# New places for the pieces between the products, zero transfers issued by SyncE, routing logits in three split parts

## Chip, cores, metric

The kernel runs as one program on 1 core of a Trainium2 chip. The metric is device time in microseconds (us); lower is better.

## The reference

Three stages follow each other. First a linear attention with decay over 4 batches, 8 heads, 768 steps, head size 48:

```
for t in range(S):
    y[t]  = r[t] @ (state + outer(u * k[t], v[t]))
    state = w[:, None] * state + outer(k[t], v[t])
```

Its output is taken as x with 3072 tokens of 384 numbers. Then a dense stage of width 2048: `x = relu(x @ w_in)**2 @ w_out`. Then a stage with 8 experts of width 1024:

```
logits = x @ w_gate
noisy  = logits + log1p(exp(x @ w_noise)) * noise
top2   = the two largest of noisy per token; their weights by softmax
out    = sum over the two: weight * (relu(x @ w1[e]) @ w2[e])
```

Everything is float32. The order of `noisy` decides where a token goes, so the logits need nearly full precision.

## The kernel before

Five engines work side by side: TensorE (PE) multiplies, VectorE (DVE), ScalarE (ACT) and GpSimd (POOL) do the rest, SyncE (SP) issues most transfers. Each executes its own instructions in the order in which the code writes them, and waits for the others by semaphores.

The dense stage runs over 6 blocks (j = 0 to 5) of 512 tokens, each in 16 steps f of 128 hidden columns. In step f, `mm1(j, f)` makes nine products of 128x512 into a `ph` bank, `gsplit` turns it into g = relu squared in a high and a low part (three ACT operations, then the DVE subtraction `gl`), and `mm2`, two steps behind (LAG = 2), makes nine products into the bank `xo`. Large products use float32 values split into a high and a low part of type fp32r, three products for one.

Between these products stand "slots", two per step: slot 2f after `mm1` and `gsplit` of step f, slot 2f + 1 after that step's `mm2`. `put(n, fn, ...)` puts a piece of other work in slot int(n); the digits behind the point order the pieces of one slot. The tables written out by hand at the top of the file give these numbers:

- `CHUNKS`: attention for the four 128-token chunks q of the next block, eleven pieces each: `pre`, `p_tr` for r and for k, `pre2`, `p_kv`, `p_a`, `p_r` twice, `p_y` twice, `p_x`. `p_y` adds into `vd` on DVE, `p_x` transposes the sum on PE (L484). The lists are for j = 0, j = 1 and j = 2 to 4. Block 5 has no attention.
- the conversion of the dense weights in block 0: piece n (0 to 15; 13 of them in the slots) takes `conv_w1` (an ACT operation), `conv_w2` (four DVE operations, L238, L239, L240, L244, then the load of piece n + 2) and `conv_w3` (an ACT copy, L252, and a POOL subtraction, L253). Piece 14 holds the weights that the `mm2` after slot 28 needs first.
- `ROUTE` and `RESTS`: the routing of block j - 1, in block j: `r_rest`, four `r_row`, the softplus, top 2, rank and eight `r_send`, which scatter the rows by an indirect transfer on POOL. Routing of block 5 stands in the first `up` pieces of the experts, by `ROUTE_LAST`.

`r_row` transposes 128 tokens (three products with `ident`, L559), multiplies them with the gates in plain float32 (L562), copies the logits out on DVE (L564) and the row on ACT (L565, tile `row`), all from one PSUM bank of a ring of three. `finish` copies the block's result to the tile `x2T` on ACT and DVE before that. `rest(eng, out, src)`, used by the attention (L325, L326), subtracts the upper bfloat16 half of a float32 from it and then the upper half of what is left.

`zeros(e)` clears the expert's rows of the buffer `sent` with one transfer of 896 rows of 1,572 bytes, eight in all, in block 1. The experts follow, `up` and `down` pieces on PE, with the weights loaded and split ahead.

Of the kernel before, what the change touches and what calls it, by code (L numbers as in the profile page):

```python
# [10 lines left out]
BF = mybir.dt.bfloat16  # L11
I32 = mybir.dt.int32
AF = mybir.ActivationFunctionType
OP = mybir.AluOpType
AX = mybir.AxisListType
PSUM = bass.MemoryType.PSUM
DRAM = bass.MemoryType.DRAM
P = 128
# [8 lines left out]

CHUNKS = (((0, 1.01, 2.02, 1.03, 3.04, 2.05, 4.06, 4.07, 6.08, 7.09, 8.1),  # L30
# [11 lines left out]
RESTS = (3.4, 3.7, 5.1, 5.2)  # L42

ROUTE = ((5, 6.71, 6.72, 6.73, 6.74, 7.75, 8.76, 9.77, 9.771, 11.27, 12.78, 14.79, 13.8, 17.81, 18.82, 19.83, 20.84,
          25.15, 26.86, 26.87, 27.88),
         (4.7, 6.71, 6.72, 6.73, 6.74, 7.75, 8.76, 9.77, 9.771, 11.27, 12.78, 14.79, 13.8, 17.81, 18.82, 19.83,
          20.84, 24.85, 26.86, 26.87, 27.88),
         (5, 6.21, 6.72, 6.73, 6.74, 6.75, 7.76, 8.77, 8.771, 8.772, 11.78, 12.09, 12.8, 13.81, 13.82, 14.83, 15.84,
          15.85, 15.86, 14.87, 16.88))


ROUTE_LAST = (0.6, 0.6, 0.8, 1.81, 1.8, 1.81, 2.8, 2.81, 2.82, 3.3, 3.8, 4.8, 5.3, 5.81, 4.8, 5.8, 8.8, 7.82, 10.8,
# [11 lines left out]
def body(ctx, tc, r, k, v, w, u, w_in, w_out, w_gate, w_noise, noise, w1, w2, out):  # L64
    nc = tc.nc
# [3 lines left out]
    E, _, F2 = w1.shape  # L69
    NT = B * S  # L70
    KD = DM // P
# [7 lines left out]
    NB = NT // BLK  # L79
# [4 lines left out]
    CAP = NA * P  # L84
    PAD = E * CAP
    UNITS = ((0, 4), (4, 7))
    LAST = UNITS[-1][1]
# [4 lines left out]
    def pool(name, side="left", stack=ctx, **kw):  # L92
        return stack.enter_context(tc.tile_pool(name=name, bufs=1, side=side, reuse_waits="tile", **kw))

    consts = pool("consts")
    eb = pool("eb", side="right")
    dram = pool("dram", space=DRAM)
    sent = dram.tile([PAD + P, XW], F32, name="sent")


    C = {}
# [35 lines left out]
    def bank(tag="att", bufs=3):  # L137
        return ps.tile([P, 512], F32, name=tag, tag=tag, bufs=bufs)
# [118 lines left out]
    pb = bank()  # L257
# [37 lines left out]
    def zeros(e):  # L295
        if e == 0:
            C["zero"] = eb.tile([P, XW], F32, name="zero", tag="s3", bufs=1)
            nc.vector.memset(C["zero"], 0.0)
            nc.vector.tensor_copy(C["zero"][:, XW - 1:], C["part"])
            nc.scalar.dma_start(sent[PAD:, :], C["zero"])  # L300
        nc.scalar.dma_start(sent[e * CAP:e * CAP + LAST * P, :].rearrange("(q p) x -> p q x", p=P),
                            C["zero"][:, None, :].to_broadcast([P, LAST, XW]))

    def zero_out():
# [10 lines left out]
    def upper(ap):  # L315
        return halves(ap)[..., 1]

    def lower(ap):
        return halves(ap)[..., 0]

    def halves(ap):
        return ap.bitcast(BF).rearrange("... (x two) -> ... x two", two=2)

    def rest(eng, out, src):
        eng.tensor_tensor(out, src, upper(src), op=OP.subtract)  # L325
        eng.tensor_tensor(lower(out), out, upper(out), op=OP.subtract)  # L326
# [168 lines left out]
    X2 = {}  # L495

    def mm1(j, f):
        ph = PH[j, f] = bank("ph", 2)
        qi, fo = divmod(f, NF // NP)
        sl = slice(fo * P, (fo + 1) * P)  # L500
        n = 0
        for d in range(KD):
            for wt, xt in ((wih, x1h), (wih, x1l), (wil, x1h)):
                nc.tensor.matmul(ph, wt[qi][:, d, sl], xt[j][:, d, :], start=(n == 0), stop=(n == 3 * KD - 1))  # L504
                n += 1
# [33 lines left out]
    def small(name, shape, dt=F32, bufs=1):  # L539
        return eb.tile([P] + shape, dt, name=name, bufs=bufs)  # L540

    def r_rest(j, i):
        s = RT.setdefault(j, {})
        if i == 0:
            s["row"] = eb.tile([P, TPB, XW], F32, name="row", tag="s6", bufs=2)
            s["noise"] = small("noise", [TPB, E])
            nc.sync.dma_start(s["noise"], noise.rearrange("(q p) e -> p q e", p=P)[:, j * TPB:(j + 1) * TPB, :])

    def r_part(s, i):
        return s["row"][:, i, :DM].rearrange("p (d x) -> p d x", x=P)  # L550

    def r_row(j, i):
        s = RT[j]
        if i == 0:
            s["lz"] = small("lz", [TPB, 2 * E])
        pb = bank()
        x = X2[j][:, :, i * P:(i + 1) * P]
        for d in range(KD):
            nc.tensor.transpose(pb[:, d * P:(d + 1) * P], x[:, d, :], ident)  # L559
        lz = pb[:, KD * P:KD * P + 2 * E]  # L560
        for d in range(KD):
            nc.tensor.matmul(lz, x[:, d, :], C["gates"][:, 0, d, :], start=(d == 0), stop=(d == KD - 1),  # L562
                             skip_group_check=True)
        nc.vector.tensor_copy(s["lz"][:, i, :], lz)  # L564
        nc.scalar.copy(r_part(s, i), pb[:, :KD * P].rearrange("p (d x) -> p d x", x=P))  # L565
        if i == TPB - 1:
            s["lz"] = s["lz"].rearrange("p i (c e) -> p i c e", c=2)

# [388 lines left out]
    AW = 3  # L957
# [31 lines left out]
    for j in range(NB):  # L989
        slots = [[] for _ in range(2 * NF)]  # L990

        def put(n, fn, *args):
            k = int(n)
            slots[k].append((n - k, len(slots[k]), lambda: fn(*args)))

        if j + 1 < NB:
            for i, at_ in enumerate(CHUNKS[min(j, 2)]):
                q = (j + 1) * TPB + i
                todo = [(pre, ()), (p_tr, "r"), (p_tr, "k"), (pre2, ()), (p_kv, ()), (p_a, ()), (p_r, (0,)),
                        (p_r, (1,)), (p_y, (0,)), (p_y, (1,)), (p_x, ())]  # L1000
                for n, (fn, args) in zip(at_, todo):
                    if q > TPB or fn not in (pre, p_tr):
                        put(n, fn, q, *args)
        if j == 0:
            put(0.6, conv_w3, 2)
            for n in range(AW, 2 * NP):
                m = 2 * (n - AW)
                put(m + 0.6, conv_w1, n)
                put(m + 1.6, conv_w2, n)
                put(m + 2.6, conv_w3, n)  # L1010
            put(30.6, load_routing)
        if j == 1:
            for e in range(E):
                put(e + 0.6, zeros, e)
        if j == 2:
            put(2.6, zero_out)
        if j:
            plan = [(r_row, i) for i in range(TPB)] + [(fn,) for fn in (r_soft1, r_soft2, r_soft3, r_top1, r_top2, r_sel, r_w1, r_rank, r_w2)]
            plan += [(r_send, *divmod(i, 2)) for i in range(2 * TPB)]
            for n, (fn, *args) in zip(ROUTE[0 if j == 1 else 1 if j < NB - 1 else 2], plan):  # L1020
                put(n, fn, j - 1, *args)
            for i, n in enumerate(RESTS):
                put(n, r_rest, j - 1, i)
        if j == NB - 1:
            put(4.8, f1_open)
            put(4.8, load_e, 0, 0)
            put(20.8, fetch, 0, 0)
            for n in range(NW):
                put(8.8 + 4 * n, conv_e, 0, n)
                if n + 1 < NW:  # L1030
                    put(8.8 + 4 * n, load_e, 0, n + 1)
            for c in range(KD):
                put(24.8 + 2 * c, turn, 0, 0, c)
            put(30.9, fetch, 1, 0)
        slots = [[p for *_, p in sorted(s, key=lambda x: x[:2])] for s in slots]
        for f in range(NF):
            mm1(j, f)
            gsplit(j, f)
            for p in slots[2 * f]:
                p()  # L1040
            g = j * NF + f - LAG
            if g >= 0:
                mm2(*divmod(g, NF))
                if f == LAG - 1:
                    finish(j - 1)
            for p in slots[2 * f + 1]:
                p()
# [116 lines left out]
```

## Time and profile before

| what | us |
|---|---|
| median of 3 timed runs | 1044.29 |
| lowest and highest of them | 1041.76, 1044.68 |
| the profiled execution's own time | 1036.84 |
| its span from the first to the last instruction | 1035.0 |
| PE busy | 996.3 |
| DVE, ACT, POOL busy | 585.1, 418.5, 397.6 |

The span is what the trace's views cut up; 1.8 us of the execution lie outside it. Busy time of PE is modelled, so its share says where PE pauses, not how near it is to its peak. Granted clock 1.00 is the level of 2.4 GHz; the mean of the run is 0.983. In the views a row names the line of the kernel, the engine, the operation and the tiles as out<-in; idle time stands behind it with what ended it.

### The profile page before, as it was taken

The page shows a single profiled execution, that of the slowest core. Times are in us where ns is not written, and L with a number is a line of the kernel's source. Part 1 is how long each engine was busy: PE and PEld are TensorE (multiplying, and loading weights), DVE is VectorE, ACT ScalarE, POOL GpSimd, SP SyncE. Part 2 cuts the span into 40 slices and gives each one's busy share as a digit, 9 for nine tenths or more (in the row PEclk, how much of TensorE's full clock was granted, in tenths as well). Part 3 has the DMA queues.
Part 4 walks back from the last instruction along what each step waited for, and adds up shares of the span by engine and source line. Part 5 has one row for each costly group of instructions (what it writes and reads, how often), then busy time and mean ns, then how long its engine had stood idle before and what let it go on. Part 6 is the DMA issues. An engine that isn't in the chain of part 4 may idle for free.

```text
span 1035.0 us, 15948 instructions
## 1 busy us (share of the span) xinstructions
PE 996.3 (96%) x6023; PEld 880.0 (85%) x6023; DVE 585.1 (57%) x1070; ACT 418.5 (40%) x731; POOL 397.6 (38%) x435
## 2 busy tenths in 40 slices
PE   8887998999999999999999999999999999999995
PEld 8766876888888888888888899999999898989894
DVE  8998955755964774685254463554545454444320
ACT  2445543334434433443465542443434334434320
POOL 7544543574485467547111253122120312112121
PEclk9888998999999999999999999999999999999998
DMA  8444369446452224322013567376555455554121
GB/s 191 132 136 137 107 181 348 114 106 198 104 126 76 59 67 106 68 64 64 24 58 82 139 142 166 83 141 129 104 104 113 89 117 99 110 98 79 20 32 22
DMA packets 193287, 112.25 MB, mean 108 GB/s; under 512 B 131632, under 2 KB 185776, under 8 KB 193200
## 3 DMA queue, kind: packets, MB, share of 16 engines
q1 hardware_dynamic: 174336, 79.75, 31.9%
q0 software_dynamic: 10624, 19.89, 10.6%
q10 hardware_dynamic: 8240, 11.49, 3.3%
q8 instruction: 49, 0.80, 0.3%
q14 instruction: 38, 0.31, 0.1%
HBM read 74.83 MB, written 36.27 MB: 107 GB/s over the span
## 4 chain that ended last, share of the span: by engine, by line
PE 74%; DVE 15%; ACT 3%; issue 3%; POOL 2%; DMA 1%; ACTq 1%; SPq 0%; DVEq 0%; POOLq 0%
PE ph L798 21%; PE y L819 14%; PE ph L504 13%; PE xo L527 12%; PE y L847 7%; DVE gl L516 2%; DVE t L238 1%; PE att L388 1%; DVE t L240 1%; DVE t L239 1%; DVE am L392 1%; PE att L449 1%; DVE vd L453 1%; DVE t L244 1%; ACT rt L510 1%
## 5 line engine op out<-in xcount | busy, mean ns | idle before, releaser
L830 POOL DMA_INDIRECT out<-yt,id x56 | 87.3, 1559 | 334.1 <-ACT yt L828 291.9
L516 DVE TENSOR_TENSOR gl<-g,gh 128x512 fp32r<-128x512 f32 x96 | 72.2, 752 | 154.8 <-ACT gh L514 154.6
L805 DVE SCALAR_TENSOR_TENSOR hl<-ph,hh 128x512 fp32r<-128x512 f32 (+1 forms) x128 | 75.4, 590 | 145.8 <-ACT hh L804 145.7
L798 PE MATMUL ph<-xh,w0h 128*128 128x320 f32 (+1 forms) x384 | 136.7, 356 | 0.0
L798 PE MATMUL ph<-xh,w0l 128*128 128x320 f32 (+1 forms) x384 | 134.9, 351 | 0.0
L798 PE MATMUL ph<-xl,w0h 128*128 128x320 f32 (+1 forms) x384 | 134.7, 351 | 0.0
L510 ACT ACTIVATE rt<-ph 128x512 f32<-128x512 f32 x96 | 57.1, 595 | 183.4 <-PE ph L504 172.7
L504 PE MATMUL ph<-x1h,wih 128*128 128x512 f32 x288 | 118.9, 413 | 0.0
L527 PE MATMUL xo<-gh,woh 128*128 128x512 f32 x288 | 117.2, 407 | 0.1
L504 PE MATMUL ph<-x1l,wih 128*128 128x512 f32 x288 | 114.5, 398 | 0.0
L504 PE MATMUL ph<-x1h,wil 128*128 128x512 f32 x288 | 114.0, 396 | 0.0
L527 PE MATMUL xo<-gh,wol 128*128 128x512 f32 x288 | 113.3, 393 | 0.0
L527 PE MATMUL xo<-gl,woh 128*128 128x512 f32 x288 | 113.1, 393 | 0.0
L804 ACT ACTIVATE hh<-ph 128x512 fp32r<-128x512 f32 (+1 forms) x128 | 66.1, 517 | 106.3 <-PE ph L798 103.7
L819 PE MATMUL y<-w1h,hh 128*128 128x384 f32 (+1 forms) x280 | 93.7, 335 | 0.0
L819 PE MATMUL y<-w1h,hl 128*128 128x384 f32 (+1 forms) x280 | 93.6, 334 | 0.0
L819 PE MATMUL y<-w1l,hh 128*128 128x384 f32 (+1 forms) x280 | 93.6, 334 | 0.0
L798 PEld LDWEIGHTS ph<-xh,w0l 128*128 128x128 f32 x384 | 72.1, 188 | 8.3
L798 PEld LDWEIGHTS ph<-xl,w0h 128*128 128x128 f32 x384 | 72.2, 188 | 7.2
L798 PEld LDWEIGHTS ph<-xh,w0h 128*128 128x128 f32 x384 | 72.2, 188 | 7.1
L690 POOL DMA_INDIRECT sent<-row,si x48 | 50.2, 1045 | 51.5 <-ACT gh L514 42.4
L779 DVE TENSOR_TENSOR xl<-xt,xh 128x512 fp32r<-128x512 f32 (+1 forms) x48 | 28.4, 592 | 70.3 <-ACT xh L778 70.3
(206 smaller groups left out, 2185.2 us busy)
## 6 DMA issues: line engine op xcount, KB each, us to landing
ws<-in_moe_w SPq DMA_DIRECT2D x128, 96.0 KB, 2.7
ws<-in_moe_w SPq DMA_DIRECT2D x32, 384.0 KB, 3.3
sent<-zero ACTq DMA_DIRECT2D x8, 1375.5 KB, 16.6
G<-sent SPq DMA_DIRECT2D x36, 192.0 KB, 4.7
stg<-in_moe_w_in SPq DMA_DIRECT2D x8, 768.0 KB
stg<-in_moe_w_out SPq DMA_DIRECT2D x8, 768.0 KB, 4.6
out<-zero SPq DMA_DIRECT2D x1, 4800.0 KB, 15.4
lv<-in_v SPq DMA_DIRECT2D x24, 192.0 KB, 2.9
```

The lines of the kernel that those rows point to most:

```text
L504: nc.tensor.matmul(ph, wt[qi][:, d, sl], xt[j][:, d, :], start=(n == 0), stop=(n == 3 * KD - 1))
L510: nc.scalar.activation(rt, ph, AF.Relu)
L516: nc.vector.tensor_tensor(gl, g, gh.bitcast(F32), op=OP.subtract)
L527: nc.tensor.matmul(XO[j][:, d, :], wt[qi][:, fo, sl], gt, start=(f == 0 and n == 0), stop=(f == NF - 1 and n == 2))
L690: st = nc.gpsimd.indirect_dma_start(out=sent, in_=s["row"][:, i, :], in_offset=None, out_offset=bass.IndirectOffsetOnAxis(ap=s["si"][:, i, ...
L779: nc.vector.tensor_tensor(xl[:, c, :], xt, xh[:, c, :].bitcast(F32), op=OP.subtract)
L798: nc.tensor.matmul(ph, wt[:, d, sl], xt[:, d, :], start=(m == 0), stop=(m == 3 * KD - 1))
L804: nc.scalar.activation(hh[:, :n], ph, AF.Relu)
L805: nc.vector.scalar_tensor_tensor(hl[:, :n], ph, 0.0, hh[:, :n].bitcast(F32), op0=OP.max, op1=OP.subtract)
L819: nc.tensor.matmul(py, ht[:, sl], wt[:, fo, :], start=(m == 0), stop=(m == 3 * NF2 - 1))
L830: st = nc.gpsimd.indirect_dma_start(out=out, in_=yt, in_offset=None, compute_op=OP.add, out_offset=bass.IndirectOffsetOnAxis(ap=IDX[e, un] ...
L847: nc.tensor.matmul(py, wt[:, fo, sl], ht[:, :n], start=(m == 0), stop=(m == 3 * NF2 - 1))
```

## The change

New numbers for all slots of the attention, the weight conversion (each of its three parts has a number of its own), the routing and the remainders; both transfers of `zeros` issued by SP, in other slots; and the logits as sums of bfloat16 products. The gates are split once into three bfloat16 parts on POOL (`r_gates`). x is split by `rest` on DVE into the tile `row`, which later takes the row itself. For each of three groups of 128 values there are three products, of 48, 32 and 16 columns; a DVE reduction adds the three groups of 16 columns.

```diff
@@ tables
-CHUNKS = (((0, 1.01, 2.02, 1.03, 3.04, 2.05, 4.06, 4.07, 6.08, 7.09, 8.1),
...
+CHUNKS = (((0.05, 18.86, 0.12, 1.28, 1.7, 0.25, 19.07, 17.86, 2.8, 8.59, 10.62),
+           (1.04, 2.39, 2.87, 11.49, 15.14, 13.05, 12.05, 12.97, 15.15, 16.74, 20.072),
+           (8.9, 10.05, 11.36, 17.63, 17.78, 19.46, 27.09, 24.81, 21.09, 21.79, 26.6),
+           (19.9, 21.94, 23.95, 24.44, 28.47, 24.05, 9.45, 25.8, 28.24, 28.66, 30.23)),
+          ((0.61, 1.15, 1.62, 4.46, 0.92, 4.53, 8.04, 4.78, 9.71, 9.79, 16.75),
+           (8.19, 8.45, 9.21, 10.83, 11.37, 15.55, 15.56, 17.25, 20.81, 22.05, 24.32),
+           (12.48, 15.01, 17.33, 23.4, 25.4, 22.07, 22.34, 22.43, 25.71, 26.15, 28.23),
...
+CONV_AT = ((2.51, 3.49, 5.37),
+           (3.77, 5.56, 6.06),
+           (5.6, 5.79, 6.86),
...
+           (25.17, 25.63, 27.03),
+           (26.63, 27.52, 29.74))
-RESTS = (3.4, 3.7, 5.1, 5.2)
+RESTS = ((3.08, 3.67, 5.03, 7.89),
+         (3.12, 4.23, 4.81, 5.34),
+         (4.06, 5.62, 6.85, 6.88))
...
+ROUTE = ((6.82, 6.85, 7.86, 9.71, 10.44, 11.12, 11.54, 12.03, 12.901, 14.64, 17.23, 17.43, 18.16,
+          27.26, 18.48, 29.39, 18.42, 18.97, 26.19, 31.66, 31.81),
+         (4.66, 6.71, 7.02, 7.36, 8.46, 9.44, 9.66, 10.95, 11.671, 12.52, 14.9, 17.36, 17.83,
+          17.86, 19.95, 29.56, 30.15, 25.55, 26.8, 26.64, 30.69),
...
@@ zeros
-            nc.scalar.dma_start(sent[PAD:, :], C["zero"])
-        nc.scalar.dma_start(sent[e * CAP:e * CAP + LAST * P, :].rearrange("(q p) x -> p q x", p=P),
+            nc.sync.dma_start(sent[PAD:, :], C["zero"])
+        nc.sync.dma_start(sent[e * CAP:e * CAP + LAST * P, :].rearrange("(q p) x -> p q x", p=P),
@@ routing
+    def r_gates():
+        g = C["gates"]
+        rest(nc.gpsimd, g[:, 1], g[:, 0])
+        C["gates3"] = consts.tile([P, KD, 3, 2 * E], BF, name="gates3")
+        for n, t in enumerate((upper(g[:, 0]), upper(g[:, 1]), lower(g[:, 1]))):
+            nc.gpsimd.tensor_copy(C["gates3"][:, :, n, :], t)
...
     def r_rest(j, i):
...
+        rest(nc.vector, r_part(s, i), X2[j][:, :, i * P:(i + 1) * P])
...
-        lz = pb[:, KD * P:KD * P + 2 * E]
+        lz = pb[:, KD * P:KD * P + 6 * E].rearrange("p (g e) -> p g e", g=3)
         for d in range(KD):
-            nc.tensor.matmul(lz, x[:, d, :], C["gates"][:, 0, d, :], start=(d == 0), stop=(d == KD - 1),
-                             skip_group_check=True)
-        nc.vector.tensor_copy(s["lz"][:, i, :], lz)
-        nc.scalar.copy(r_part(s, i), pb[:, :KD * P].rearrange("p (d x) -> p d x", x=P))
+            for n, t in enumerate((upper(x[:, d, :]), upper(xr[:, d, :]), lower(xr[:, d, :]))):
+                nc.tensor.matmul(lz[:, n:], t, C["gates3"][:, d, :3 - n, :], start=(d == 0 and n == 0),
+                                 stop=(d == KD - 1 and n == 2), skip_group_check=True)
+        nc.vector.tensor_reduce(s["lz"][:, i, :], lz.rearrange("p g e -> p e g"), axis=AX.X, op=OP.add)
+        nc.scalar.copy(xr, pb[:, :KD * P].rearrange("p (d x) -> p d x", x=P))
@@ main loop
-                m = 2 * (n - AW)
-                put(m + 0.6, conv_w1, n)
-                put(m + 1.6, conv_w2, n)
-                put(m + 2.6, conv_w3, n)
+                for at_, fn in zip(CONV_AT[n - AW], (conv_w1, conv_w2, conv_w3)):
+                    put(at_, fn, n)
...
+            put(2.9, r_gates)
             for e in range(E):
-                put(e + 0.6, zeros, e)
+                put(e * 3 // 2 + 3.6, zeros, e)
```

## Rows read from the trace of the kernel before

**Rows 1.** The page's busy table: us (share of the span) xinstructions.
```profile
PE 996.3 (96%) x6023; PEld 880.0 (85%) x6023; DVE 585.1 (57%) x1070; ACT 418.5 (40%) x731; POOL 397.6 (38%) x435
```

**Rows 2.** Busy time by stretch; blocks 0, 1, 2, 5, then experts; columns in first line.
```profile
core 0: us, PE busy (x) PEld busy (x) DVE busy (x) ACT busy (x) POOL busy (x), PEclk, DMA share, GB/s
37.00:138.40 101.40, 90.41 (x484) 74.70 (x483) 89.38 (x99) 53.51 (x84) 50.12 (x34) 0.91 0.45 125
138.40:236.40 98.00, 91.50 (x588) 76.19 (x588) 56.56 (x121) 35.80 (x64) 53.06 (x57) 0.97 0.66 191
236.40:325.00 88.60, 87.67 (x589) 73.23 (x588) 57.15 (x122) 35.60 (x64) 52.28 (x55) 1.00 0.49 134
...
500.50:570.20 69.70, 69.70 (x328) 57.78 (x327) 28.56 (x78) 38.86 (x66) 9.31 (x15) 1.00 0.21 55
570.20:600.00 29.80, 29.80 (x160) 25.84 (x160) 17.14 (x53) 16.67 (x30) 7.41 (x6) 1.00 0.54 130
600.00:1010.00 410.00, 410.00 (x2387) 386.97 (x2386) 191.93 (x299) 155.62 (x283) 93.38 (x122) 1.00 0.51 102
```

**Rows 3.** Waits of PE, whole run: us in total, times, longest us.
```profile
PE att L484 <- DVE vd L425: 10.1, 2, 5.8
```

**Rows 4.** Timeline of ACT in block 1: start us, us, instruction [idle before <-releaser].
```profile
162.76 4.18 ACTq L301 DMA_DIRECT2D sent<-zero  x1
...
166.98 0.48 ACT L565 COPY row<-att 128x384 f32<-128x384 f32 x1 [3.08 <-DVE lv L326]
```

**Rows 5.** Timeline of PE in block 1.
```profile
167.51 1.17 PE L437 MATMUL att<-Z,rT 112*128 112x96 f32 x4 [4.85 <-ACT row L565]
```

**Rows 6.** Timeline of PE in block 5: gate products, then the next row.
```profile
516.42 0.74 PE L562 MATMUL att<-gates,x2T 128*128 128x16 f32 x6
517.01 0.52 PE L559 MATMUL att<-ident,x2T 128*128 128x128 f32 x3
```

**Rows 7.** Timeline of PE in block 5: the rank piece and what follows.
```profile
531.28 0.19 PE L663 MATMUL att<-sel,mask 128*128 128x32 bf16 x1
531.32 0.18 PE L665 MATMUL att<-pre,ones 128*128 128x32 bf16 x1
531.35 0.17 PE L667 MATMUL att<-tot,ones 128*128 128x8 bf16 x1
531.37 0.48 PE L527 MATMUL xo<-gh,woh 128*128 128x512 f32 x1
531.69 0.40 PE L527 MATMUL xo<-gl,woh 128*128 128x512 f32 x1
531.92 0.39 PE L527 MATMUL xo<-gh,wol 128*128 128x512 f32 x1
```

**Rows 8.** DMA queues from 146 to 185 us: packets, MB, share of 16 engines.
```profile
q10 hardware_dynamic: 7440, 11.47, 86.4%
```

**Rows 9.** Groups of DVE instructions, whole run: xcount | busy us, mean ns | idle before.
```profile
L326 DVE TENSOR_TENSOR lv<-lv 128x384 bf16<-128x384 f32 x16 | 9.6, 598 | 0.5
L325 DVE TENSOR_TENSOR lv<-lv 128x384 f32<-128x384 f32 x16 | 8.8, 550 | 0.0
```

**Rows 10.** Groups of POOL instructions in block 0.
```profile
L253 POOL TENSOR_TENSOR wol<-t,woh 128x768 fp32r<-128x768 f32 x8 | 15.0, 1881 | 24.4 <-ACT woh L252 24.4
```

**Rows 11.** Groups of DVE instructions in block 0.
```profile
L238 DVE TENSOR_SCALAR t<-t 128x768 f32<-128x768 f32 x14 | 19.4, 1388 | 4.0 <-ACT t L231 4.0
L240 DVE SCALAR_TENSOR_TENSOR t<-stg,t 128x768 int32<-128x768 int32 x14 | 17.0, 1214 | 0.5
L244 DVE SCALAR_TENSOR_TENSOR t<-stg,t 128x768 int32<-128x768 int32 x14 | 15.5, 1105 | 0.5
L239 DVE TENSOR_SCALAR t<-t 128x768 int32<-128x768 int32 x14 | 13.6, 975 | 0.5
```

**Rows 12.** Timeline of DVE in block 0: its first gl, the last conversion's last operation.
```profile
43.08 0.69 DVE L516 TENSOR_TENSOR gl<-g,gh 128x512 fp32r<-128x512 f32 x1 [0.45 <-ACT gh L514]
...
130.69 0.96 DVE L244 SCALAR_TENSOR_TENSOR t<-stg,t 128x768 int32<-128x768 int32 x1
```

**Rows 13.** One line, L238: duration ns min/median/max, first and last start us.
```profile
L238 DVE TENSOR_SCALAR t<-t x16: 542/1485/2183, 23.8 to 126.9; 128x768 f32<-128x768 f32 x16
```

More of the change, by code (lines that the diff above doesn't have):

```diff
@@ L25 @@
 CONV = {2: 0, 3: 1}
-CHUNKS = (((0, 1.01, 2.02, 1.03, 3.04, 2.05, 4.06, 4.07, 6.08, 7.09, 8.1),
[11 rows of a table removed]
-RESTS = (3.4, 3.7, 5.1, 5.2)
[L44 to L49, printed above, removed]
+CHUNKS = (((0.05, 18.86, 0.12, 1.28, 1.7, 0.25, 19.07, 17.86, 2.8, 8.59, 10.62),
[11 rows of a table added]
+CONV_AT = ((2.51, 3.49, 5.37),
+           (3.77, 5.56, 6.06),
+           (5.6, 5.79, 6.86),
+           (7.44, 7.69, 8.35),
+           (8.33, 9.36, 11.19),
+           (9.67, 11.86, 13.47),
+           (12.66, 13.68, 15.85),
+           (15.34, 15.72, 16.16),
+           (17.06, 17.88, 18.34),
+           (19.88, 19.95, 21.52),
+           (21.26, 23.6, 24.17),
+           (25.17, 25.63, 27.03),
[4 more added lines that the diff above has]
+ROUTE = ((6.82, 6.85, 7.86, 9.71, 10.44, 11.12, 11.54, 12.03, 12.901, 14.64, 17.23, 17.43, 18.16,
[5 rows of a table added]
 ROUTE_LAST = (0.6, 0.6, 0.8, 1.81, 1.8, 1.81, 2.8, 2.81, 2.82, 3.3, 3.8, 4.8, 5.3, 5.81, 4.8, 5.8, 8.8, 7.82, 10.8,
@@ L556, in r_row @@
         pb = bank()
-        x = X2[j][:, :, i * P:(i + 1) * P]
+        x, xr = X2[j][:, :, i * P:(i + 1) * P], r_part(s, i)
         for d in range(KD):
             nc.tensor.transpose(pb[:, d * P:(d + 1) * P], x[:, d, :], ident)
-        lz = pb[:, KD * P:KD * P + 2 * E]
+        lz = pb[:, KD * P:KD * P + 6 * E].rearrange("p (g e) -> p g e", g=3)
         for d in range(KD):
-            nc.tensor.matmul(lz, x[:, d, :], C["gates"][:, 0, d, :], start=(d == 0), stop=(d == KD - 1),
-                             skip_group_check=True)
-        nc.vector.tensor_copy(s["lz"][:, i, :], lz)
-        nc.scalar.copy(r_part(s, i), pb[:, :KD * P].rearrange("p (d x) -> p d x", x=P))
+            for n, t in enumerate((upper(x[:, d, :]), upper(xr[:, d, :]), lower(xr[:, d, :]))):
[3 more added lines that the diff above has]
+        nc.scalar.copy(xr, pb[:, :KD * P].rearrange("p (d x) -> p d x", x=P))
         if i == TPB - 1:
@@ L1021, in body @@
                 put(n, fn, j - 1, *args)
-            for i, n in enumerate(RESTS):
+            for i, n in enumerate(RESTS[0 if j == 1 else 1 if j < NB - 1 else 2]):
                 put(n, r_rest, j - 1, i)
```

18 rows, old and new, of tables (CHUNKS, ROUTE) are left out of this document.

## The prediction, made before the change was run

> **What bounds the kernel now.** I read the page's busy table first: TensorE (PE) is busy 96% of the span [rows 1]. A share that high hides stages with different limits, so the next view was the table of busy time by stretch, cut at the first product of each 512-token block [rows 2]. The reader is to see four things there. From 600 us to 1010 us PE never pauses, and block 5 and the stretch after it are full too. Block 2 idles 0.93 us in 88.6. Block 0 lasts 101.4 us with PE busy 90.4 at a granted clock of 0.91, and VectorE (DVE) busy 89.4: it is the one block that DVE sets. Block 1 does the same work as block 2 and lasts 98.0, 9.4 us longer, at clock 0.97. So there are three places to win or lose: block 0, the 9.4 us of block 1, and PE's own work everywhere else. Which wait ends last in each came from the waits of PE: its longest is the transposes of p_x (L484) for the sum `vd` (L425) that stands behind the weight conversions in DVE's queue [rows 3]. In block 1 the timeline shows ScalarE (ACT) held by its own transfer issues: one `sent<-zero` issue takes 4.18 us, the row copy waiting behind it starts at 166.98, and PE, which needs that copy's PSUM bank, idles 4.85 us until 167.51 [rows 4, 5]. PE then pays again: clock 0.97 over 98 us is 2.9 us of work lost, where block 2 has 1.00 [rows 2].
>
> **Gate products.** Each of 24 row pieces now multiplies x with the gates in true float32: three products in the source, six records in the trace. They run from 516.42 to 517.01, 0.59 us [rows 6]. The change has nine bf16 products of 48, 32 or 16 columns. The nearest bf16 rows are those of the rank piece: from start to start 0.03 us and 0.02 us at 32 columns, and 0.02 us at 8 [rows 7]; the width does not show, so nine cost some 0.23. The first float32 product behind them takes 0.32 instead of 0.23 to the next one: 0.09 more, and the way in a further 0.01 [rows 7]. So 0.59 becomes 0.33, and 24 x 0.26 = 6.2 us goes, nearly all in blocks where PE is the bound. Ends: without the 0.09 it is 24 x 0.36 = 8.6; with it paid twice 24 x 0.17 = 4.1. I take 6.2, the row's own pattern.
>
> A rule of the Trainium skill speaks against this term: "TensorE: Matmul & The Clock Gate", section "LDWEIGHTS (loading the stationary operand)", gives a weight load about P/1.2 ns for P columns, an estimate of 107 ns for 128 columns whatever they hold. The six float32 records agree with it (590/6 = 98 ns). Nine loads by it would be 0.96 us, and the edit would cost 24 x 0.37 = 9 us in place of gaining 6. The bf16 rows, at 20 to 30 ns with a 128-column load each, say otherwise [rows 7], and the same page's fast weight load for types other than fp32 goes with them.
>
> **The zero transfers.** They leave ACT's queue for SyncE's (SP's) and go from slots 0.6 to 7.6 to slots 3.6 to 13.6. ACT loses the blocked issues, and with them the wait that ends last in block 1. I set the block to block 2's 88.6: 9.4 us gone. Bounds: 0, if the wait only changes its engine, and 10.3, if block 2's 0.93 of idle goes as well. The transfers are no smaller: ACT's queue moved 11.47 MB from 146 to 185 us [rows 8], so about 3 MB per 10 us, and the engines were full. What is behind the zeros on SP? In issue order it is the noise load, zeros 0 to 3, the load of k for chunk 11, then r and the eight turned loads for chunk 10. SP does not keep step with PE, so the first four (each 896 rows of 1,572 bytes, 1.4 MB; together some 19 us) go in one burst from slot 3.6, about 8 us into the block, to about 27 us. The loads behind them cannot start before about then anyway: they wait for DVE's transposes of chunk 9 in slots 8 and 9. Their first user is chunk 10 in slots 12 to 15, about 36 to 43 us in. Chunk 9's loads are issued at slot 1.6, ahead of every zero. That is the cover; without it the queue of loads slips by up to 4 us for each zero before it.
>
> The Trainium skill, "DMA: Bandwidth & Descriptors", section "Issuing engines are not separate DMA queues", says that the issuer changes only who spends the issue time, on the same 16 engines. By that rule the 9.4 us come back only so far as the issue on ACT was the cause, which the 4.85 us wait supports; the rest is the second rival below.
>
> **DVE's remainders.** r_rest now has two subtractions for each of the 24 row pieces. Operations of the same 128x384 shapes take 0.55 and 0.60 us [rows 9]: 4.6 us a block, 27.6 in all. In blocks 1 to 4 DVE rises from some 57 to 62 us of 88, in block 5 from 29 to 33 of 70, in the first `up` pieces (570 to 600 us) from 17 to 22 of 30 [rows 2]. The cost is nothing on PE as long as that idle time covers it; the first of them waits for ACT's last copy of x2T, behind it stand the chunk's mask products and `gl`, and PE's row piece comes one and a half slots later. The reduction that replaces the copy of `lz`, and five small GpSimd operations once, stay under 1 us off the path; at the price of GpSimd's 1.88 us subtraction [rows 10] the five would be 9.4 us of a GpSimd that has 45 idle us in block 1 [rows 2].
>
> **New places in block 0.** No work goes away. A conversion's four DVE operations are 1.39 + 0.98 + 1.21 + 1.11 = 4.69 us [rows 11], and 13 of them (61 us) with some 27 us of attention work and `gl` fill DVE. PE cannot pass slot 28 before the weights of piece 14 are converted. Summing DVE's work slot by slot at those durations, the old order has 77.6 us up to that conversion (slot 23) and 84.9 to the last one (slot 25); the new has 79.1 (slot 25) and 85.1 (slot 27). Both start from the first `gl` at 43.1 [rows 12]. In the old order the last conversion ends at 131.65 [rows 12]: 43.1 + 84.9 = 128.0, so 3.7 us of gaps, and PE needs 6.7 us more. In the new order the first conversion comes later (slot 3, not 1), but a(4), kv(4) and a transposed chunk are done in that time; I count 0.6 us lost. The last conversion ends at 43.7 + 85.1 = 128.8 without gaps. `gl`, Z and `vd` are 2 us more, then the transposes of p_x (0.5), and nine products at 0.23 (2.1): 133.4. The weights of piece 14, converted by 122.8 and finished by a ScalarE copy and GpSimd's 1.88 [rows 10], come earlier than that. The p_x pieces now stand two slots behind their y where it was one, which attacks the 10.1 us of rows 3. Gaps of 1.6, somewhat under half of the old, give 135.0, a gain of 3.4 us. Bounds: if half of the excess of the conversions over the shortest run of one (0.54 for the first operation [rows 13], so at least 0.85 x 13 = 11) goes too, the gain is some 9; if the gaps double to 7.4, the block ends at 140.8, a loss of 2.4.
>
> **Blocks 2 to 5 and after** keep their PE work but for the gates. Block 2's idle 0.93 is all that new places can win there; late remainders can cost as much. I take zero. The rest of the program has the old code.
>
> **Sum.** 6.2 + 9.4 + 3.4 = 19.0 us. The profiled execution took 1036.84 us (span 1035.0 and 1.8 around it), so its like would take 1017.8. The timed runs lie at 1041.76 to 1044.68, median 1044.29, that is 7.4 above the profiled one; carried over, the forecast is 1025.3, so 1025.
>
> **Rivals.**
> 1. Block 0 is won more fully: fewer conversions run beside GpSimd's work, and PE's clock stays up. For it: the first operation ranges from 0.54 to 2.18 us [rows 13]. Against: GpSimd's subtraction still follows each conversion. Gain 9 more: 1016. Chance 0.17.
> 2. The loads queue behind the zeros on SP and block 1 keeps its length, the wait moved from ACT to DVE's transposes. For: full transfer engines [rows 8]. Against: the order of issue above. 1025 + 9.4 = 1034. Chance 0.14.
> 3. Slower: the remainders come too late. DVE takes them in order behind ACT's copy; if PE reaches its first row piece before they are done, it waits up to 4.6 us in each of blocks 1 to 5, 23 us, 4 more than the sum: 1048. It decides from the point where DVE is over 4 us behind PE in slot 4. Against: DVE has 31 us to spare in block 2 [rows 2]. Chance 0.07.
> 4. The change does not do what it says: gates cost as much as before (0.59) and block 1's wait moves, leaving block 0 alone: within 0.3%, about 1042. Chance 0.05.
>
> The forecast has 0.57, with 1018 to 1033 as its own range. The range of 1012 to 1039 takes in the first two rivals and their unknowns and leaves out the last two and the tails, some 0.18. What a measurement of this kernel can tell from no change is 0.3%, 3.1 us. Faster: 0.57 + 0.17 + 0.14 = 0.88; same 0.05; slower 0.07.
>
> **What would show it.** In the profile after: bf16 gate products at 20 to 30 ns from start to start, and a row piece 0.26 us shorter; no ACT issue of zeros, block 1 near 88 us with clock 1.00; block 0 near 98; DVE busier by some 27 us in all with PE idle in blocks 2 to 5 under 1 us each. The prediction is wrong if row pieces wait for remainders, if block 1's first 40 us hold a PE wait for a transposed chunk, or if block 0 keeps its 101.

## The result, and the profile after

The changed kernel takes 1029.63 us (median of 4 runs, 1029.01 to 1030.97) where the kernel before takes 1043.56 (4 runs, 1041.76 to 1044.68): a ratio of 0.987, 95% interval 0.985 to 0.989, 13.9 us faster. The forecast was 1025, so 19 us; the time lies inside the range. The profiled execution after has a span of 1027.2, 7.8 less than the profiled one of before.

Busy time by stretch after, cut as in [rows 2]: blocks 0, 1, 2, 5, the first expert pieces, the experts behind them (us, PE, PEld, DVE, ACT, POOL, granted clock, DMA share, GB/s):

```profile
37.00:132.00 95.00, 89.55 (x484) 72.67 (x482) 86.26 (x99) 54.23 (x84) 48.63 (x33) 0.94 0.44 128
132.00:226.50 94.50, 88.11 (x601) 73.47 (x600) 65.90 (x131) 35.52 (x63) 56.83 (x63) 0.98 0.72 202
226.50:315.50 89.00, 86.83 (x600) 72.00 (x601) 62.76 (x130) 35.76 (x63) 52.74 (x56) 1.00 0.48 134
...
488.90:563.80 74.90, 73.43 (x358) 59.52 (x358) 33.50 (x87) 38.89 (x67) 9.49 (x17) 1.00 0.25 62
563.80:603.10 39.30, 36.88 (x220) 32.55 (x219) 31.16 (x76) 19.86 (x34) 14.06 (x12) 1.00 0.53 126
603.10:1000.00 396.90, 395.62 (x2307) 373.42 (x2305) 183.14 (x281) 152.01 (x276) 88.52 (x116) 1.00 0.52 101
```

The next table cuts every kernel of this study at the same products: a block runs from its first product to the next block's; "experts 1" is the first expert's `up` pieces and its first `down`, where the last routing stands.

```
us                     blk0   blk1   blk2   blk3   blk4   blk5  experts1   rest*    span
before                101.4   98.0   88.6   87.2   88.3   73.8    37.3    423.3   1035.0
after                  95.1   94.4   89.0   86.8   86.7   74.9    39.3    424.1   1027.2
a0_changed_again       94.3   95.2   89.8   86.8   86.6   75.9    40.5    423.8   1031.4
e1_zero_behind_v       94.5   90.7   88.0   85.8   86.7   75.1    40.4    424.4   1025.6
e2_zeros_on_act        94.8   97.1   88.1   85.8   86.6   75.4    40.4    424.1   1030.3
e3_old_gates           94.5   91.9   87.7   86.5   87.4   78.0    37.3    423.5   1024.7
e4_sends_early         94.5   95.1   88.1   85.8   86.6   75.4    40.3    424.0   1027.4
b1_block0_places       94.2  100.0   89.7   89.1   89.3   73.8    37.3    423.3   1034.1
b2_split_gates_alone  100.7   98.7   91.0   90.6   91.1   72.4    40.6    422.6   1045.5
b3_zeros_on_sp_alone  101.3   94.7   89.6   89.0   89.4   73.8    37.3    423.3   1035.4
c1_three_waits_mended  94.0   90.6   89.1   86.9   86.6   72.4    41.0    424.0   1021.5
c2_old_gates_mended    94.6   91.9   89.5   87.6   87.8   73.8    37.3    423.5   1022.4
d1_old_gates_last      94.2   91.2   89.9   86.9   86.6   72.4    37.3    422.8   1018.1
d2_no_gpsimd_split     94.0   90.5   89.8   87.5   86.6   72.4    41.1    423.6   1022.9
* what follows experts 1; ahead of block 0 lie 36.4 to 39.9 us
```

So block 0 gave 6.3 us and block 1 only 3.6; blocks 2 to 4 together 1.6; block 5 lost 1.1, experts 1 lost 2.0 and the rest 0.7. The waits of PE after (us in total, times, longest) name the losses. The 10.1 us of [rows 3] are gone; the 3.5 us of `xo` for `woh` and `wol` are new, in block 0, where `mm2` waits for its first converted weights:

```profile
PE att L688 <- DVE am L408: 4.7, 1, 4.7
...
PE att L583 <- ACT row L590: 2.8, 4, 0.9
PE xo L543 <- ACT woh L268: 2.2, 1, 2.2
...
PE xo L543 <- POOL wol L269: 1.3, 1, 1.3
...
PE att L587 <- DVE row L342: 1.2, 2, 0.8
```

**Block 1.** SP's timeline after (start us, us, instruction): the first four zero transfers go in one burst, as forecast, but the fifth stands ahead of the load of v for chunk 10.

```profile
147.04 7.15 SPq L317 DMA_DIRECT2D sent<-zero  x4
...
169.52 0.43 SPq L317 DMA_DIRECT2D sent<-zero  x1
170.05 0.51 SPq L183 DMA_DIRECT2D lv<-in_v  x1
170.60 2.00 SPq L317 DMA_DIRECT2D sent<-zero  x1
```

DVE takes its instructions in order, and the routing chain that PE's rank piece (L688) needs stands behind v's subtraction. DVE's timeline after, then PE's:

```profile
176.24 0.56 DVE L341 TENSOR_TENSOR lv<-lv 128x384 f32<-128x384 f32 x1 [4.55 <-DMA lv<-in_v]
...
182.22 0.16 DVE L656 TENSOR_TENSOR tot<-pre,sel 128x8 bf16<-128x8 bf16 x1
```

```profile
183.99 0.18 PE L688 MATMUL att<-sel,mask 128*128 128x32 bf16 x1 [4.72 <-DVE am L408]
...
185.03 0.63 PE L520 MATMUL ph<-x1h,wih 128*128 128x512 f32 x1
185.46 0.63 PE L520 MATMUL ph<-x1l,wih 128*128 128x512 f32 x1
```

The releaser that the waits name is `am`, the next operation in DVE's queue behind `tot`, probably for the PSUM bank that it reads; all of this queue stands back by the 4.55 us for v. Behind the pause two products start 0.43 us apart instead of 0.23, at the lower clock level, 1.2 GHz: the mean granted clock from 184 to 188 us is 0.58.

**Gate products.** PE's timeline in block 5 after: nine bf16 products, and the products that follow them; then a float32 row piece of before in the same place.

```profile
511.91 0.19 PE L587 MATMUL att<-gates,x2T 128*128 128x48 bf16 x1
511.93 0.20 PE L587 MATMUL att<-gates,row 128*128 128x32 bf16 x2
...
512.09 0.20 PE L587 MATMUL att<-gates,row 128*128 128x32 bf16 x2
512.14 0.47 PE L520 MATMUL ph<-x1h,wih 128*128 128x512 f32 x1
512.45 0.39 PE L520 MATMUL ph<-x1l,wih 128*128 128x512 f32 x1
```

```profile
513.34 0.74 PE L562 MATMUL att<-gates,x2T 128*128 128x16 f32 x6
513.93 0.48 PE L504 MATMUL ph<-x1h,wih 128*128 128x512 f32 x1
514.24 0.40 PE L504 MATMUL ph<-x1l,wih 128*128 128x512 f32 x1
```

Nine take 0.23 us, 25 ns from start to start, in place of the 0.59 of [rows 6]. The first large product behind them takes 0.31 to the next one instead of 0.23, but so does the one behind the float32 gate products of before (513.93 to 514.24). So a row piece gains 0.36, not the 0.26 of the forecast, which charged that step to the new products alone. Block 5 bears it out: where PE does not pause, it takes 73.8 us with old gates (before) and 72.4 with split ones (b2, c1, d1), and 4 x 0.36 = 1.4. The 107 ns that the prediction worked out from "TensorE: Matmul & The Clock Gate" of the Trainium skill, section "LDWEIGHTS (loading the stationary operand)", is not what such a product costs here: the record of each of these weight loads lasts 0.10 us, but they start 25 ns apart.

**Remainders.** Groups of DVE after, whole run: the same shapes as [rows 9], at a mean of 0.73 and 0.82 us, and up to 1.4 and 2.1.

```profile
L342 DVE TENSOR_TENSOR row<-row 128x384 bf16<-128x384 f32 x24 | 19.6, 816 | 0.8
L341 DVE TENSOR_TENSOR row<-x2T 128x384 f32<-128x384 f32 x24 | 17.6, 733 | 3.3 <-ACT x2T L550 3.3
```

**Block 5.** The expert's fetch of its rows (SP's timeline) is issued at 542.86, and DVE waits for it:

```profile
542.86 2.71 SPq L786 DMA_DIRECT2D G<-sent  x4
```

```profile
549.61 1.06 DVE L801 STREAM_TRANSPOSE xt<-G 128x512 f32<-128x512 f32 x1 [3.76 <-DMA G<-sent]
```

### The profile page after: what moved, and what is told of

Same layout as the page of the kernel before. It is cut to its first block, busy times and chain, and to the rows that moved or that the text cites. A ratio compares the mean times of both kernels' runs of the same rounds, so it can differ in the third digit from the quotient of the medians.

```text
span 1027.2 us, 16145 instructions
## 1 busy us (share of the span) xinstructions
PE 986.9 (96%) x6095; PEld 868.5 (85%) x6095; DVE 623.2 (61%) x1118; ACT 419.9 (41%) x731; POOL 406.4 (40%) x440
## 4 chain that ended last, share of the span: by engine, by line
PE 77%; DVE 10%; issue 4%; ACT 3%; DMA 2%; POOL 2%; SPq 1%; another core or an unknown queue 0%; ACTq 0%; DVEq 0%; POOLq 0%
PE ph L823 19%; PE ph L520 16%; PE y L844 14%; PE xo L543 13%; PE y L872 6%; PE att L404 2%; PE att L465 1%; DVE t L254 1%; DVE gl L532 1%; DVE t L256 1%; DVE t L255 1%; PE att L453 1%; PE att L482 1%; DMA ws<-in_moe_w 1%; ACT rt L526 1%
## 5 line engine op out<-in xcount | busy, mean ns | idle before, releaser
L532 DVE TENSOR_TENSOR gl<-g,gh 128x512 fp32r<-128x512 f32 x96 | 82.3, 857 | 106.8 <-ACT gh L530 95.3
L715 POOL DMA_INDIRECT sent<-row,si x48 | 49.9, 1039 | 64.8 <-ACT w0h L763 41.1
```

Of the source, the lines that this page charges most:

```text
L532: nc.vector.tensor_tensor(gl, g, gh.bitcast(F32), op=OP.subtract)
L715: st = nc.gpsimd.indirect_dma_start(out=sent, in_=s["row"][:, i, :], in_offset=None, out_offset=bass.IndirectOffsetOnAxis(ap=s["si"][:, i, ...
```

## The experiments

Theory after the result: the mechanisms of the forecast work, and three new waits take some 10 us back: v behind a zero transfer in block 1, remainders of the split gates on a DVE that shares time with GpSimd, and a late fetch in block 5. Rivals: ACT's freedom comes from the spread slots, not from the new issuer; the split gates gain and the places alone lose; the profiled before is not typical of its timed runs. Ratios are to the kernel before, run beside each group. In the group of e1 to e4 that kernel took 1037.03 (1036.33 to 1038.47), not 1043 to 1044 as in the others, so those four are compared with each other.

**e1.** Zero transfers 4 to 7 go behind the load of v in their slots.

```
-                put(e * 3 // 2 + 3.6, zeros, e)
+                put(e * 3 // 2 + (3.6 if e < 4 else 3.85), zeros, e)
```

> Zeros 4 to 7 stand behind the v load of chunk 10 in SyncE's order (slot 9.85 instead of 9.6); nothing else is changed. Theory: in the changed kernel VectorE waited 4.55 us for that v load, which stood behind zero 4, the routing chain behind it was late, and TensorE waited 4.72 us at the rank piece and then ran at half clock. Then the wait at the rank goes and block 1 (94.5 us) falls to 88 to 90, the time to 1024. Rival: the rank is late because VectorE has 4.6 us of remainders more in front of it; then block 1 keeps 94 us and the time 1029.6.

Measured 1026.56, ratio 0.989 (0.988 to 0.991). The forecast of this run was a little too good (88 to 90 and 1024). DVE's wait for v and PE's for the rank in e1:

```profile
176.49 0.56 DVE L341 TENSOR_TENSOR lv<-lv 128x384 f32<-128x384 f32 x1 [2.39 <-DMA lv<-in_v]
```

```profile
PE att L688 <- DVE am L408: 1.4, 1, 1.4
```

Block 1 falls to 90.7, against 95.1 in e4, whose block 1 is the changed kernel's; timed, e1 is 3.9 below e4. In the changed kernel, four transfers' place in SP's queue cost about 4 us.

**e2.** The changed kernel with the same slots, the zeros issued by ACT.

```
-            nc.sync.dma_start(sent[PAD:, :], C["zero"])
+            nc.scalar.dma_start(sent[PAD:, :], C["zero"])
```

(and the same for the main transfer.)

> The changed kernel with the zero transfers issued by ScalarE again, in the new slots. Theory: the issuing engine is what mattered in block 1, so ScalarE is held by issues of up to 4 us again and block 1 is 98 us or more, the time 1033 or more. Rival: the new slots alone, spread over 11 instead of 8, free ScalarE, and the loads on SyncE no longer stand behind zeros: block 1 at 90 or less, the time 1025.

Measured 1031.42, ratio 0.994 (0.993 to 0.996). ACT's timeline, then DVE's, in e2:

```profile
158.58 0.71 ACTq L317 DMA_DIRECT2D sent<-zero  x1
...
177.57 0.99 ACTq L317 DMA_DIRECT2D sent<-zero  x2
```

```profile
180.31 1.41 DVE L341 TENSOR_TENSOR lv<-lv 128x384 f32<-128x384 f32 x1 [5.65 <-DMA lv<-in_v]
```

An issue holds ACT 0.4 to 0.7 us, not the 4.18 of [rows 4]: the later slots, spread over 11 instead of 8, freed ACT, whoever issues the transfers. v is late all the same, by 5.65, though no zero stands ahead of it in SP's queue: SP issues it at 176.74 (170.05 after), and its own waits put 4.6 us before that down to zero transfers. So each was half right: ACT is free, as the rival had it, and block 1 is as long as the theory nearly had it, from another cause. "DMA: Bandwidth & Descriptors" of the Trainium skill, section "Issuing engines are not separate DMA queues", has the issuer change only who spends the issue time; e2 agrees, 1031.4 against the 1030.4 of e4, where SP issues.

**e3.** The changed kernel with the float32 gate product of before and without remainders.

```
-        rest(nc.vector, r_part(s, i), X2[j][:, :, i * P:(i + 1) * P])
...
-            for n, t in enumerate((upper(x[:, d, :]), upper(xr[:, d, :]), lower(xr[:, d, :]))):
...
+            nc.tensor.matmul(lz, x[:, d, :], C["gates"][:, 0, d, :], start=(d == 0), stop=(d == KD - 1),
```

> The changed kernel with the float32 gate products and no remainders; places and zeros as changed. Theory: 24 row pieces are 0.36 us longer on TensorE (8.6 us), and the waits that remainders bring go (0.6 to 0.8 us a block in blocks 2 to 4, 2.0 in the experts' first pieces, something in block 1): net 2 to 4 us slower than the changed kernel, 1032 to 1034. Rival: VectorE's 27.6 us of remainders cost as much as the products give, so the time stays at 1029 or falls.

Measured 1026.70, ratio 0.990 (0.989 to 0.992): 3.7 us below e4, where the theory wanted it slower. Against e4 it wins 3.2 in block 1 and 3.0 in experts 1 and loses 0.7 and 0.8 in blocks 3 and 4 and 2.6 in block 5. In the changed kernel the split gates cost more than they bring. In block 1 the wait at the rank is nearly gone, with v still behind the fifth zero transfer:

```profile
PE att L686 <- DVE am L408: 1.5, 1, 1.5
```

That is the rival of e1, remainders ahead of the rank in DVE's queue. Each of the two, moving v (e1, 90.7) or taking the remainders away (e3, 91.9), mends most of block 1; both together (c2, 91.9) bring no more than e3 alone. The loss needed both.

**e4.** Block 5's eight sends in slots 15.6 to 17.1 instead of 16.5 to 20.4.

> The changed kernel with the eight sends of block 5 in slots 15.6 to 17.1 instead of 16.5 to 20.4. Theory: the last send set the start of the first fetch, so the turned tokens came late (VectorE waited 3.76 us for G, ScalarE 5.58 behind it) and the last products of the dense stage lost 2.4 us: the time falls by 2 to 2.5 us to 1027.3. Rival: the fetch is limited by the transfers themselves or the wait costs TensorE nothing: 1029.6.

Measured 1030.43, ratio 0.994 (0.992 to 0.995). The first send starts 41.6 us into the block, as it did after, the fetch is issued at 54.1 (after: 53.9), and DVE still waits for it in e4:

```profile
548.92 1.06 DVE L801 STREAM_TRANSPOSE xt<-G 128x512 f32<-128x512 f32 x1 [4.25 <-DMA G<-sent]
```

The theory falls in this form: the new slots did not move the sends at all, presumably because the top-2 and rank pieces before them still stand at slots 14.98 and 15.16.

**a0.** The changed kernel again.

> The changed kernel again, unaltered, on the chip of the runs it is compared with. Both theories: ratio to the kernel before 0.987 as first measured. Rival: the ratio depends on how slow the first blocks of the kernel before are on that chip (its time was 1043.6 in one call and 1037.0 in the next), then 0.992 to 0.994.

Measured 1032.09 (1030.0 to 1033.17), ratio 0.988 (0.987 to 0.990): the result repeats. A before near 1037, the rival's condition, did not come up beside it.

**b1.** The kernel before with the changed `CHUNKS[0]` and `CONV_AT` alone.

> The kernel before with the new places of block 0 alone (attention chunks 4 to 7 and the conversions). Theory: the 6.3 us by which block 0 became shorter (101.4 to 95.1) come from these places: block 0 at 95, block 1 at 98, time 6 us below before. Rival: block 0 gained from something else, as an other state of TensorE's clock; then under 3 us.

Measured 1036.82, ratio 0.994 (0.992 to 0.995): block 0 at 94.2, so its gain comes from these places. DVE's conversions in block 0, in the changed kernel (xcount, busy, mean ns, idle before):

```profile
L256 DVE SCALAR_TENSOR_TENSOR t<-stg,t 128x768 int32<-128x768 int32 x14 | 16.0, 1146 | 0.5
L254 DVE TENSOR_SCALAR t<-t 128x768 f32<-128x768 f32 x14 | 15.7, 1122 | 1.4 <-ACT t L247 1.4
L255 DVE TENSOR_SCALAR t<-t 128x768 int32<-128x768 int32 x14 | 14.8, 1060 | 0.5
L260 DVE SCALAR_TENSOR_TENSOR t<-stg,t 128x768 int32<-128x768 int32 x14 | 14.8, 1058 | 0.5
```

They sum to 4.39 us a conversion where [rows 11] have 4.69: 14 x 0.30 = 4.1 us; and the idle time ahead of the first operation is 1.4 instead of 4.0. But `gl` got longer (a mean of 0.82 instead of 0.68) and waits more (5.9 instead of 1.3), so this is not the block's gain. PE's own account is: of 101.4 and 95.0 us it idles 11.0 before and 5.5 after, and its busy time falls from 90.4 to 89.6 at a clock of 0.94 instead of 0.91. How much of that the shorter conversions brought is not shown.

**b2.** The kernel before with split gates and remainders alone, in the old places. **b3.** The kernel before with the zeros on SP in the new slots alone.

> The kernel before with the split gates and the remainders alone. Theory: TensorE's row pieces are 0.36 us shorter, but the old places give the remainders too little time: row 0 stands at slot 4.7 with rests at 3.4 to 5.2; blocks 1 to 5 gain under 4 us, the first expert pieces lose 2 to 4: within 2 us of before. Rival: the gain is 6 us as worked out before the run.

> The kernel before with the zero transfers on SyncE in the new slots alone. Theory: ScalarE is no longer held, so the 4.85 us wait goes with its half clock; the loads of chunk 10 stand behind zeros in another order than in the changed kernel: block 1 from 98 to 89 to 92, time 6 to 9 us below before. Rival: the wait moves to the loads and block 1 stays above 95.

b2 took 1047.79, ratio 1.0035 (1.002 to 1.005): slower by 3.4 us, more than the 2 that its theory allowed. Waits of PE in b2:

```profile
PE att L571 <- DVE row L326: 7.9, 8, 1.3
...
PE att L571 <- DVE row L325: 1.8, 4, 0.6
```

Row pieces do wait for remainders there, 9.7 us in 12 waits: rival 3's mechanism, at less than half of its price. b3 took 1037.31, ratio 0.993 (0.992 to 0.995), block 1 at 94.7: between its theory and its rival. PE waits there for `vd` (3.1 us) and `kT` (1.3), and for no load. The transfers' part is worth 3.3 us of block 1 against the profile of before, 5.3 against b1's, and 7 us timed.

**c1, c2, d1, d2: mending the waits.** c1 is the changed kernel with e1's move, block 5's routing in its old slots with remainders early, and the last four remainders earlier. c2 is c1's places with e3's old gates (without that last move).

```
-         (4.06, 5.62, 6.85, 6.88))
+         (3.08, 3.1, 4.2, 4.3))
...
-         (6.42, 8.08, 8.31, 9.32, 9.72, 10.18, 10.35, 10.54, 10.581, 10.902, 12.54, 15.16, 14.98,
+         (5, 6.21, 6.72, 6.73, 6.74, 6.75, 7.76, 8.77, 8.771, 8.772, 11.78, 12.09, 12.8, 13.81, 13.82, 14.83, 15.84,
...
-ROUTE_LAST = (0.6, 0.6, 0.8, 1.81,
+ROUTE_LAST = (0.6, 0.6, 0.61, 0.62,
```

> The changed kernel with three small moves: zeros 4 to 7 behind the v load; the routing of block 5 in the old, earlier places, with its remainders in slots 3 and 4; the remainders of the last routing issued together before the first split. Theory: three waits go: 3.7 us in block 1, 2.4 at the end of the dense stage (fetch later than the turn's slot because the rank stands at slot 15), 2 at the first expert pieces: 8 us below the changed kernel, 1021. Rival: GpSimd still stretches VectorE's remainders (2.11 us for one of 0.60) and the fetch is late for another reason: only block 1 gains, 1025.

> The changed kernel with float32 gates and no remainders, zeros 4 to 7 behind the v load, block 5's routing in the old places. Theory: with the waits mended the split gates are worth their 6 us on TensorE, so this one is 3 to 6 us slower than the one with split gates and the same moves. Rival: remainders cost what the products give, so both are within 1 us or this one is faster.

Both took 1025.0 (1025.05 and 1024.97, both 0.982, 0.981 to 0.984). That is the time of both rivals, though c1 mended block 5 as well as block 1; only experts 1 did not gain. The fetch in block 5 is issued 48.7 us into the block in c1 instead of 53.9, and the block falls to 72.4. Between c1 and c2, split gates win 5.0 us in blocks 1 to 5 (20 row pieces at 0.36 are 7.2; PE waits 2.0 for row copies, L583, that c2 does not have) and lose 3.7 in experts 1. There PE waits 3.4 us for remainders and row copies in c1, and the granted clock of the stretch is 0.96; in c2 it never pauses there and has 1.00. Why the remainders are late: GpSimd's timeline in c1, then DVE's.

```profile
559.56 6.26 POOL L764 TENSOR_TENSOR w1l<-ws,w1h 128x768 fp32r<-128x768 f32 x3 [29.42 <-ACT w1h L763]
```

```profile
559.85 2.20 DVE L341 TENSOR_TENSOR row<-x2T 128x384 f32<-128x384 f32 x1
562.08 2.07 DVE L342 TENSOR_TENSOR row<-row 128x384 bf16<-128x384 f32 x1
564.04 2.18 DVE L341 TENSOR_TENSOR row<-x2T 128x384 f32<-128x384 f32 x1
566.26 0.59 DVE L342 TENSOR_TENSOR row<-row 128x384 bf16<-128x384 f32 x1
```

As long as GpSimd's three subtractions run, each remainder lasts as long as one of them (6.26 / 3 = 2.09); the one behind them takes 0.59. d2 gives GpSimd's share of the expert weights to DVE, d1 is c1 with the old gates and no remainders in the last routing alone (and its last remainders' move undone, which is then empty).

```
-SPLIT_POOL = 4
+SPLIT_POOL = 0
```

```
-        rest(nc.vector, r_part(s, i), X2[j][:, :, i * P:(i + 1) * P])
+        if j < NB - 1:
+            rest(nc.vector, r_part(s, i), X2[j][:, :, i * P:(i + 1) * P])
...
+        if j == NB - 1:
```

> The mended version with split gates everywhere, and the low parts of the first four expert weights computed on VectorE (0.96 us each) instead of GpSimd (1.8 us). Theory: GpSimd's subtractions stretch VectorE's remainders (0.55 to 2.2 us); without them the remainders take 0.55 and 0.60, VectorE has 3.8 us more, and the first eight expert pieces take 38 to 39 us instead of 41.0. Rival: the remainders are late by their place in VectorE's queue; then with 3.8 us more work there it gets worse, 42 us or more.

> The kernel with the mended waits, split gates in blocks 1 to 5, float32 gates without remainders in the last routing alone. Theory: the split gates pay some 5 us in blocks 1 to 5 and lose 3.7 us in the experts' first pieces and 0.7 behind them, so this one is 4 us below both mended versions: 1021 where before is 1043.6, ratio 0.978. Rival: the loss in the first pieces comes from somewhere else than the last routing's remainders: 1025, ratio 0.982.

d2 took 1025.45, ratio 0.982 (0.981 to 0.984). DVE's remainders in d2 and a wait of PE:

```profile
561.97 0.55 DVE L341 TENSOR_TENSOR row<-x2T 128x384 f32<-128x384 f32 x1
562.55 0.59 DVE L342 TENSOR_TENSOR row<-row 128x384 bf16<-128x384 f32 x1
```

```profile
PE att L583 <- ACT row L590: 4.6, 4, 2.6
```

The stretching is gone and experts 1 still last 41.1, between theory and rival. The longest of these waits, 2.6, is there, and the clock of the stretch is 0.96 again; probably the row is late because DVE now has the subtractions as well, which no run tried by itself. d1 took **1020.50** (1019.85 to 1022.16), ratio **0.978 (0.977 to 0.979)**: the fastest, ahead of both kernels, where its theory had it (1021). Its blocks 1 and 5 and experts 1:

```profile
131.10:222.30 91.20, 86.98 (x601) 72.14 (x600) 63.73 (x131) 35.48 (x63) 57.09 (x62) 1.00 0.77 210
...
485.70:558.10 72.40, 72.40 (x359) 59.70 (x358) 33.37 (x87) 38.88 (x66) 8.78 (x17) 1.00 0.29 66
558.10:595.40 37.30, 37.30 (x209) 34.07 (x208) 23.90 (x68) 20.21 (x34) 13.32 (x13) 1.00 0.53 129
```

PE does not pause in the last two.

## Why the prediction was right and wrong

**Right in sign and in range, 5 us too hopeful.** The nearness is in part luck: it hides errors of both signs.

**Block 0: mis-sized, 3.4 forecast, 6.3 measured** (7.2 in b1). The term followed DVE's queue to its last conversion and had PE end 6.7 us (before) or 4.6 (new) behind it. That is not the path: PE is busy without a pause from 119 us to the block's end at 138.4 before, and from 110 to 132.0 after, where the last conversion ends at 126.7. What the places changed are PE's waits earlier in the block: the 10.1 us for `vd`, which the term named but did not add up, are gone, and 3.5 for the first converted weights came, where it counted 0.6 lost by the later start. In part this is rival 1's outcome, at 2.9 of the 9 us it was given: conversions are shorter and the clock is 0.94 instead of 0.91; its reason, fewer conversions beside GpSimd's work, was not tried by itself.

**Gates: PE's side too small, the cover wrong.** A row piece gained 0.36 us instead of 0.26, so 24 of them 8.6, the term's upper end: the 0.09 of the step behind them was there before too. The step that failed is "the cost is nothing on PE as long as that idle time covers it". It compared sums of idle time over a block, and took durations of [rows 9], where the places leave none of them stretched. A remainder needs DVE at one moment, and there it lasted up to 2.1 us. DVE's busy time rose by 38.1 us from [rows 1], not 27:

```profile
PE 986.9 (96%) x6095; PEld 868.5 (85%) x6095; DVE 623.2 (61%) x1118; ACT 419.9 (41%) x731; POOL 406.4 (40%) x440
```

That a row piece waits for a remainder, named ahead as a sign of failure, shows in the waits after (L587, 1.2 us, and L583, 2.8 for the row copy) and more in b2. PE's idle time in blocks 2, 3 and 5 is 2.2, 1.5 and 1.5 us after, where the prediction had under 1 each. Net, the split gates cost 3 to 4 us in the changed kernel (e3) and in the old places (b2), and nothing in mended places (c1 against c2); kept out of the last routing they bring some 4.5 (d1 against c2).

**Block 1: 9.4 forecast, 3.6 measured.** Taking the wait for ACT away worked. The list of loads behind the zeros named k, r and the turned ones and left out v of chunk 10, and slots 9.6 and later were not laid beside its place. So part of rival 2 came true: the wait moved to DVE, then to PE, and the clock fell again behind it. e1's one move brings the block to 90.7, two thirds of the missing 5.8. The remainders had their share: without them, and with v in the same place, PE waits 1.5 us instead of 4.7 (e3). The reason was also half right: e2 shows that the slots freed ACT, not the issuer.

**Block 5: taken as zero, lost 1.1** (2.5 behind c1's 72.4). The rank's move from slot 12.09 to 15.16 was not followed on to the fetch behind the sends.

**Profile and median.** The profiles differ by 7.8 us, the timed medians by 13.9. The profile of before lies 6.7 below its median. b1 has the code of before in blocks 1 to 4, and b3 in blocks 2 to 4, and there PE waits for `vd`; in b1:

```profile
PE att L497 <- DVE vd L466: 6.1, 8, 2.1
```

In the profile of before the same waits sum to 1.5 us, and its blocks 1 to 4 are 362.1 long where b1 has 368.1 (2.0 of it in block 1). So by the profiles the forecast's 19 us stand against 7.8, and the other 6 of the timed 13.9 are probably a cost of the old places that the profile of before did not hold; the timed runs have no profile to show it. In the group where before took 1037.03, e4 is only 6.6 below it. Taking blocks 2 to 4 as zero and carrying the difference over to the median would have left that gain out. What makes one execution of before take 1037 and another 1044 stays open.

## What to carry over

A new instruction on an in-order engine costs what it delays behind it at that moment, with the duration that it has beside the neighbour it will run beside; a block's idle sum says nothing of that. When transfers move to a queue, list every load that then stands behind one of them, with its first user, and put the long ones behind the loads of the same slot. Before charging a new instruction for a slow step behind it, look whether the old one is followed by the same step. And split a change by stage before judging it: here one edit won in five blocks and lost most of it in a sixth place.

## What the runs showed of the hardware

Beside GpSimd's subtractions of two SBUF tiles, DVE's subtraction of 128x384 took 2.07 to 2.20 us instead of 0.55 to 0.60. "SBUF — State Buffer" of the Trainium skill, section "Who interferes with whom", says that a DVE instruction with two SBUF inputs contends with a GpSimd instruction that reads SBUF, and calls the contention for the shared ports an exclusive lock; c1 and d2 agree: a stretched remainder lasts as long as one GpSimd subtraction (2.09 us), and without them it takes 0.55.

The first 128x512 product behind a row piece takes 0.31 us to the next instead of 0.23, behind bf16 gate products and behind float32 ones alike.
